# Attention output by full-width streams with ones beside V, and a new order of the first halves' work, in an attention and feed-forward kernel

## The chip, the cores and the metric

The kernel runs on one core of one Trainium2 chip. The metric is the device time of one execution in microseconds; a "fast" run is one that lies within 1.5% of the fastest run of the same kernel. Profiles are of single executions, and their span is some 1.8 us shorter than the time of that execution.

Engines: PE is TensorE, DVE VectorE, ACT ScalarE, POOL GpSimd, SP SyncE (which here only issues transfers). PSUM is the memory into which PE writes its results; a pool's "bufs" are its buffers. A crossbar transpose is a transfer that transposes on its way. PE is called cold where its groups stand about twice as far apart as elsewhere (1.28 us instead of 0.65 for a gate group).

## The reference, cut to what matters

```python
# q, k, v: (4, 8, 768, 64); 8 global keys, 96 local keys
scores = q @ k.T / 8 + bias(head, distance); masked to global | local keys
a = exp(scores - max) / sum(exp(scores - max))
x = (a @ v) regrouped to (3072, 512)
out = (relu(x @ w_gate) * (x @ w_val)) @ w_out      # 512 -> 1536 -> 512
```

The kernel cuts each of the 4 batches into two halves of 384 queries: halves 0 to 7. Chunk c of the feed-forward is half c. While PE works on the feed-forward of chunk c, the attention of half c+1 is woven in between. QK is the product of queries and keys, AV that of the weights and V. A batch's even half is called a first half, its odd half a second half.

## The kernel before

Keys are cut into tiles j of 120 keys of their own and the 8 global ones. For each pair of heads, `piece_qk` makes the unnormalised weights `es`, and `piece_av` runs twice: once with ones as the stationary operand (the sum of the weights), once with V. Each matmul fills 64 of the 128 columns of the array; the two heads of a pair stand in the two halves.

```python
def piece_av(s, p, what):
    av = av_psum.tile([128, 512], FP32, name="av_ps")          # av_psum has 2 buffers
    for i, (j, a, w, m) in enumerate(todo):                    # 4 tiles in a first half, 5 in a second
        for e in range(2):
            nc.tensor.matmul(av3[64 * e : 64 * e + 64, :, a : a + w],
                             lhsT=ones if what == 0 else vbuf[b % 2][:, j, D * h : D * h + D],
                             rhs=es[...], ...)
    if what == 0:
        nc.scalar.activation(ln, av[:, 0:QH], AF.Ln, ...)
        nc.scalar.activation(rc, ln, AF.Exp, bias=0.0, scale=-1.0)
    else:
        nc.vector.tensor_tensor(xT_of[s][:, p, :], av[:, 0:QH], av_of[s, p], op=ALU.mult)
...
# halves 0 and 1: casts, PE transposes (piece_t), copies to qT and kT
# halves 2 to 7 ("early pieces"): casts on GpSimd, crossbar transposes issued by SP, copies to kT on GpSimd
...
weave(f1_0[0:G2], [])
weave(f1_0[G2 : 2 * G2], attention_pieces(1), 0.0, 1.2)
...
weave(f1_1[0 : 2 * G2], [])
weave(f1_0[2 * G2 :] + f1_1[2 * G2 :], early_pieces(2))
weave(f2_0 + f2_1, attention_pieces(2) + early_pieces(3))
```

`weave` emits feed-forward pieces in order and puts the attention pieces between them at even distances. Every engine is given its instructions in the order of the program, so this order decides who waits for whom.

The softmax here doesn't subtract the row's maximum and nothing guards it: scores larger than these inputs give would overflow.

## Time and profile before

The time was 284.66 us in the median of four runs (284.48 to 288.38). The execution that the profile shows took 285.32 us, at a mean granted clock of 0.976.

| engine | busy, us | share of the span of 283.5 us |
|---|---|---|
| PE | 250.5 | 88% |
| PE weight loads | 138.6 | 49% |
| ACT | 147.7 | 52% |
| DVE | 123.0 | 43% |
| POOL | 93.7 | 33% |

PE's 88% is not evenly spread: from 127 us on it has no gap, before that it has holes. Two groups of the page of the kernel before give the price of what follows a pair's AV (line, engine, operation, tiles and shapes, count; then busy us and mean ns of one; then the engine's idle time before them):

```profile
L339 DVE TENSOR_TENSOR xT<-av_ps,rcp 128x384 bf16<-128x384 f32 x32 | 17.8, 555 | 37.2 <-PE av_ps L325 29.9
...
L332 ACT ACTIVATE lnd<-av_ps 128x384 f32<-128x384 f32 x32 | 15.8, 494 | 17.4 <-PE av_ps L325 17.4
```

There is one logarithm of 494 ns and one multiply of 555 ns per pair, each over all 128 partitions.

### The profile page before, as it was taken

Reading aid. Unit: us, or ns where it says so; the run is one execution under the profiler, and the core shown is the slowest. Engines: PE = TensorE matmul, PEld = TensorE weight load, DVE = VectorE, ACT = ScalarE, POOL = GpSimd, SP = SyncE. Lnnn points to the kernel's source line nnn. Section 1 sums busy time; section 2 is a strip of 40 time slices with the busy share of each in tenths; the row PEclk is TensorE's granted clock in tenths of the full one; section 3 lists DMA queues with packets and bytes.
Section 4 is the critical chain, followed back from the end, with each engine's and each line's share of the span. In section 5 each row is a group of like instructions: output and inputs, shape, how many; then the busy total and the mean of one; then the engine's idle time right before and its main releaser. Section 6 shows DMA issues by size and latency. Waiting matters only on the chain.

```text
span 283.5 us, 5047 instructions
## 1 busy us (share of the span) xinstructions
PE 250.5 (88%) x1824; PEld 138.6 (49%) x1824; DVE 123.0 (43%) x328; ACT 147.7 (52%) x301; POOL 93.7 (33%) x231
## 2 busy tenths in 40 slices
PE   1366966799989929999999999999999999999994
PEld 0134534465545415554555455554555465545551
DVE  6555266634344105652355326540664155523320
ACT  8466245833367215664565457554755376543421
POOL 8990129614280019425051631434140300000000
PEclk9997799999999986999999999999999999999999
DMA  7999990998412379747454397348845110011002
GB/s 199 170 204 193 228 237 9 109 287 233 102 39 75 93 190 261 96 109 77 131 172 112 96 148 226 69 100 118 259 58 112 74 39 1 2 62 49 2 22 89
DMA packets 81200, 34.38 MB, mean 121 GB/s; under 512 B 56920, under 2 KB 78104, under 8 KB 81176
## 3 DMA queue, kind: packets, MB, share of 16 engines
q1 hardware_dynamic: 49320, 26.16, 32.9%
q0 software_dynamic: 31856, 7.91, 28.0%
q8 instruction: 14, 0.23, 0.3%
q14 instruction: 10, 0.08, 0.1%
HBM read 28.38 MB, written 6.29 MB: 122 GB/s over the span
## 4 chain that ended last, share of the span: by engine, by line
PE 77%; ACT 7%; DMA 6%; DVE 4%; SPq 3%; issue 1%; POOL 0%; ACTq 0%; DVEq 0%; POOLq 0%
PE ff_ps L375 21%; PE ff_ps L384 21%; PE ff_ps L365 21%; PE av_ps L325 8%; PE qk_ps L298 6%; DMA ks<-in_k_dram 5%; ACT es L301 2%; SPq L271 1%; ACT m_all L208 1%; DVE es L310 1%; SPq L274 1%; DMA kN<-kc 1%; SPq L111 1%; DVE qT L258 1%; ACT lnd L332 1%
## 5 line engine op out<-in xcount | busy, mean ns | idle before, releaser
L375 PE MATMUL ff_ps<-xT,wv 128*128 128x384 bf16 x384 | 80.7, 334 | 0.0
L365 PE MATMUL ff_ps<-xT,wg 128*128 128x384 bf16 x384 | 80.4, 332 | 0.1
L377 DVE TENSOR_TENSOR ht<-ff_ps,grelu 128x384 bf16<-128x384 f32 x96 | 53.3, 555 | 49.2 <-PE ff_ps L375 44.1
L368 ACT ACTIVATE grelu<-ff_ps 128x384 bf16<-128x384 f32 x96 | 47.1, 491 | 48.5 <-PE ff_ps L365 24.6
L384 PE MATMUL ff_ps<-wo_sb,ht 128*128 128x512 bf16 x288 | 67.9, 380 | 0.0
L310 DVE TENSOR_TENSOR es<-es,m_all 128x432 bf16<-128x432 bf16 (+6 forms) x144 | 43.4, 331 | 54.3 <-ACT es L301 52.9
L301 ACT ACTIVATE es<-qk_ps 128x432 bf16<-128x432 f32 (+2 forms) x96 | 49.4, 530 | 23.5 <-PE qk_ps L298 22.0
L298 PE MATMUL qk_ps<-qT,kT 128*128 128x432 bf16 (+6 forms) x144 | 33.9, 304 | 20.7 <-DVE kT L239 8.2
L375 PEld LDWEIGHTS <-wv 128*128 128x128 bf16 x384 | 37.1, 100 | 26.6 <-issue 3.9
L365 PEld LDWEIGHTS <-wg 128*128 128x128 bf16 x384 | 36.3, 99 | 24.6 <-issue 1.8
L384 PEld LDWEIGHTS <-ht 128*128 128x128 bf16 x288 | 26.0, 98 | 28.8
L339 DVE TENSOR_TENSOR xT<-av_ps,rcp 128x384 bf16<-128x384 f32 x32 | 17.8, 555 | 37.2 <-PE av_ps L325 29.9
L389 ACT COPY osb<-ff_ps 128x512 f32<-128x512 f32 x24 | 14.1, 586 | 30.2 <-PE ff_ps L384 30.2
L265 POOL CAST qz<-qs 128x192 bf16<-128x192 f32 x48 | 16.6, 373 | 36.1 <-issue 20.7
L298 PEld LDWEIGHTS <-kT 128*128 128x128 bf16 x144 | 14.0, 101 | 29.5 <-issue 10.0
L332 ACT ACTIVATE lnd<-av_ps 128x384 f32<-128x384 f32 x32 | 15.8, 494 | 17.4 <-PE av_ps L325 17.4
L131 POOL DMA_DIRECT2D vbuf<-in_v_dram x28 | 24.4, 883 | 0.0
L241 POOL COPY kT<-kN 128x240 bf16<-128x240 bf16 x12 | 5.0, 418 | 39.8 <-DMA kN<-kc 39.8
L325 PEld LDWEIGHTS <-ones 128*64 128x64 bf16 x288 | 11.4, 113 | 13.4 <-issue 12.7
L334 ACT ACTIVATE rcp<-lnd 128x384 f32<-128x384 f32 x32 | 16.7, 523 | 1.0
L325 PE MATMUL av_ps<-es,vbuf 128*64 128x216 bf16 (+6 forms) x288 | 15.7, 237 | 1.6 <-ACT lnd L332 1.2
L325 PEld LDWEIGHTS <-vbuf 128*64 128x64 bf16 x288 | 11.6, 114 | 10.1 <-issue 10.1
(60 smaller groups left out, 105.9 us busy)
## 6 DMA issues: line engine op xcount, KB each, us to landing
out_dram<-osb SPq DMA_DIRECT2D x24, 256.0 KB, 2.0
qs<-in_q_dram SPq DMA_DIRECT2D x6, 768.0 KB, 5.9
ks<-in_k_dram SPq DMA_DIRECT2D x6, 768.0 KB, 6.5
vbuf<-in_v_dram POOLq DMA_DIRECT2D x24, 120.0 KB, 4.4
qs<-in_q_dram SPq DMA_DIRECT2D x8, 192.0 KB, 12.8
ks<-in_k_dram SPq DMA_DIRECT2D x8, 192.0 KB, 4.7
wg<-in_moe_w_gate_dram POOLq DMA_DIRECT2D x3, 512.0 KB, 8.2
wv<-in_moe_w_val_dram POOLq DMA_DIRECT2D x3, 512.0 KB, 10.0
```

The source lines that it names most:

```text
L131: nc.gpsimd.dma_start(out=v_dst(b, NG, NG + n, j), in_=v[b, :, KT * j : KT * j + n, :].rearrange("h p d -> p h d"))
L298: nc.tensor.matmul(ps[:, c : c + n_], lhsT=kt[:, j, :], rhs=qd[:, :, :, a : a + w], start=True, stop=True)
L301: nc.scalar.activation(es[:, 0:cols], ps[:, 0:cols], AF.Exp, bias=0.0, scale=scale)
L310: nc.vector.tensor_mul(e4, e4, mk)
L325: nc.tensor.matmul(av3[64 * e : 64 * e + 64, :, a : a + w], lhsT=ones if what == 0 else vbuf[b % 2][:, j, D * h : D * h + D], rhs=es[:, ce ...
L332: nc.scalar.activation(ln, av[:, 0:QH], AF.Ln, bias=0.0, scale=1.0)
L339: nc.vector.tensor_tensor(xT_of[s][:, p, :], av[:, 0:QH], av_of[s, p], op=ALU.mult)
L365: nc.tensor.matmul(psg[:, 0:QH], lhsT=w_of(wg, dc, fc), rhs=xT[:, dc, :], start=(dc == 0), stop=(dc == N_DC - 1))
L368: nc.scalar.activation(gr, psg[:, 0:QH], AF.Relu, bias=0.0, scale=1.0)
L375: nc.tensor.matmul(psv[:, 0:QH], lhsT=w_of(wv, dc, fc), rhs=xT[:, dc, :], start=(dc == 0), stop=(dc == N_DC - 1))
L377: nc.vector.tensor_tensor(ht[:, fc, :], psv[:, 0:QH], st["gr"], op=ALU.mult)
L384: nc.tensor.matmul(ps2, lhsT=ht[:, fc, n * 128 : (n + 1) * 128], rhs=wo_sb[:, fc, :], start=(fc == 0), stop=(fc == N_FC - 1))
```

## The change

Its intent: use the whole width of the array in AV from half 2 on, so that a head needs half as many matmuls; and bring the work of halves 0 to 3 into an order in which engines wait less. The core of the diff:

```diff
-    tp_psum = ... bufs=1;  qk_psum = ... bufs=2
+    qk_psum = ... bufs=3                     # transposes share it
-    vbuf = [const.tile([128, NT, DM], BF16, ...
+    vbuf = [const.tile([128, NT, (2 * H + 1) * D], BF16, ...     # ones | V0 | ones | V1 | ... | ones
...
-            eng = nc.vector if s == 0 and (i == 0 or p == 0) else nc.gpsimd
+            eng = nc.vector if s == 0 else nc.gpsimd
...
-        put_keys(nc.scalar.copy, nc.vector.tensor_copy, kt, tp[:, 1, :], half)
+        put_keys(nc.vector.tensor_copy, nc.vector.tensor_copy, kt, tp[:, 1, :], half)
...
-    def piece_av(s, p, what):
+    def piece_av(s, p, e):                   # one head, 128 columns: V and ones
+        for i, (j, a, w, m) in enumerate(todo):
+            z0 = 2 * D * h + (D if e == 0 else 0)
+            nc.tensor.matmul(av3[:, :, a : a + w], lhsT=vb[:, j, z0 : z0 + 128], rhs=es[...], ...)
+        nc.scalar.activation(ln[o0 : o0 + 64], av[d0 : d0 + 64, 0:QH], AF.Ln, ...)
+        if e == 1:
+            nc.scalar.activation(rc, ln, AF.Exp, bias=0.0, scale=-1.0)
+            for e_ in range(2):
+                nc.vector.tensor_tensor(xT_of[s][r, p, :], av_of[s, p, e_][r, 0:QH], rc[r], op=ALU.mult)
+    def piece_av_wide(s, p): ...             # the old streams, for halves 0 and 1
...
-            return (C(0) + T(0) + C(1) + QK(0) + T(1) + C(2) + QK(1) + T(2) + ...
+            return (C(0) + T(0) + C(1) + T(1) + QK(0) + C(2) + T(2) + QK(1) + C(3) + T(3) + QK(2) + AW(0)
+                    + QK(3) + AW(1) + AW(2) + AW(3))
...
-    weave(f1_0[0:G2], [])
-    weave(f1_0[G2 : 2 * G2], attention_pieces(1), 0.0, 1.2)
+    weave(f1_0[G[0]], spread(attention_pieces(1), 0.1, 1.6),
+          [(0.9, lambda: load_w_group(2)), (0.95, lambda: load_w(wo_sb, moe_w_out, 0, DM))])
...
-    weave(f1_0[2 * G2 :] + f1_1[2 * G2 :], early_pieces(2))
-    weave(f2_0 + f2_1, attention_pieces(2) + early_pieces(3))
+    weave(f1_1[G[0]])
+    weave(f1_0[G[1]] + f1_1[G[1]], spread(early_pieces(2), 0.0, 1.0))
+    weave(f1_0[G[2]] + f1_1[G[2]] + f2_0 + f2_1,
+          spread(attention_pieces(2), 0.3, 0.9), spread(early_pieces(3), 0.4, 0.8))
...
+            placed.append(spread(attention_pieces(c + 1), 0.0, 0.88))
+            placed.append(spread(early_pieces(c + 2), 0.25, 0.75))
```

Cut: fills of the wider V tile with ones, moved loads and memsets.

More of the change, by code (lines that the diff above doesn't have):

```diff
@@ L73 @@
     osb_pool = ctx.enter_context(tc.tile_pool(name="osb", bufs=2))
-    tp_psum = ctx.enter_context(tc.tile_pool(name="tpps", bufs=1, space=bass.MemoryType.PSUM))
-    qk_psum = ctx.enter_context(tc.tile_pool(name="qkps", bufs=2, space=bass.MemoryType.PSUM))
+    qk_psum = ctx.enter_context(tc.tile_pool(name="qkps", bufs=3, space=bass.MemoryType.PSUM))
     av_psum = ctx.enter_context(tc.tile_pool(name="avps", bufs=2, space=bass.MemoryType.PSUM))
@@ L84 @@
     ident = const.tile([128, 128], BF16)
-    vbuf = [const.tile([128, NT, DM], BF16, name=f"vbuf{i}") for i in range(2)]
+    vbuf = [const.tile([128, NT, (2 * H + 1) * D], BF16, name=f"vbuf{i}") for i in range(2)]
     ones = const.tile([128, D], BF16)
@@ L116, in v_dst @@
     def v_dst(b, r0, r1, j):
-        return vbuf[b % 2][r0:r1, j, :].rearrange("p (h d) -> p h d", d=D)
+        t = vbuf[b % 2][r0:r1, j, D:]
+        return t.rearrange("p (h z) -> p h z", z=2 * D)[:, :, 0:D]
     def load_v_globals(b):
@@ L126, in spread_v_globals, with load_v, fill @@
             out=t[0:NG, j0:j1, :],
-            in_=t[0:NG, 0:1, :].to_broadcast([NG, j1 - j0, DM]))
-    def load_v(b, j):
-        n = min(KT, S - KT * j)
+            in_=t[0:NG, 0:1, :].to_broadcast([NG, j1 - j0, (2 * H + 1) * D]))
+    def load_v(b, j, r0=0, r1=KT):
+        n = min(r1, S - KT * j) - r0
         nc.gpsimd.dma_start(
-            out=v_dst(b, NG, NG + n, j),
-            in_=v[b, :, KT * j : KT * j + n, :].rearrange("h p d -> p h d"))
+            out=v_dst(b, NG + r0, NG + r0 + n, j),
+            in_=v[b, :, KT * j + r0 : KT * j + r0 + n, :].rearrange("h p d -> p h d"))
+    def fill(eng, i, j):
+        eng.memset(vbuf[i][:, j, :].bitcast(mybir.dt.uint32), 0x3F803F80)
     def load_v_half(s):
@@ L166 @@
     nc.vector.memset(ones, 1.0)
-    nc.vector.memset(vbuf[0][:, NT - 1, :], 0.0)
+    fill(nc.vector, 0, 0)
     dd = setupp.tile([128, 2, NN, WQ], FP32)
@@ L200 @@
     nc.vector.tensor_scalar(dd[0:NG, 0], gd, BIG, float(NL), op0=ALU.mult, op1=ALU.max)
-    for p in range(HP):
-        nc.vector.memset(kT[0][p][:, 3, 32:128], 0.0)
     for p in range(2):
@@ L248, in piece_t @@
         qk = cast_of[s, p]
-        tp = tp_psum.tile([128, 2, QH], BF16, name="tp")
+        tp = qk_psum.tile([128, 512], FP32, name="qk_ps")
+        tp = tp[:, 0:QH].bitcast(BF16).rearrange("d (i t) -> d i t", i=2)
         for i in range(2):
@@ L312, in piece_qk @@
             c += n_
-    def piece_av(s, p, what):
+    def piece_av(s, p, e):
         b, half = divmod(s, 2)
+        h = 2 * p + e
+        vb = vbuf[b % 2]
         av = av_psum.tile([128, 512], FP32, name="av_ps")
+        av_of[s, p, e] = av
         av3 = av[:, 0:QH].rearrange("d (n p) -> d n p", n=NN)
@@ L321, in piece_av @@
             es, c = es_of[s, p, j]
-            for e in range(2):
-                h = 2 * p + e
-                ce = c + e * NN * w
-                nc.tensor.matmul(av3[64 * e : 64 * e + 64, :, a : a + w],
-                                 lhsT=ones if what == 0 else vbuf[b % 2][:, j, D * h : D * h + D],
-                                 rhs=es[:, ce : ce + NN * w].rearrange("k (n p) -> k n p", n=NN),
-                                 start=(i == 0), stop=(i == len(todo) - 1),
-                                 skip_group_check=True)
@@ L330, in piece_av @@
-        if what == 0:
-            ln = rc_pool.tile([128, QH], FP32, name="lnd")
-            nc.scalar.activation(ln, av[:, 0:QH], AF.Ln, bias=0.0, scale=1.0)
+            c += e * NN * w
+            z0 = 2 * D * h + (D if e == 0 else 0)
+            nc.tensor.matmul(av3[:, :, a : a + w],
+                             lhsT=vb[:, j, z0 : z0 + 128],
+                             rhs=es[:, c : c + NN * w].rearrange("k (n p) -> k n p", n=NN),
+                             start=(i == 0), stop=(i == len(todo) - 1),
+                             skip_group_check=True)
@@ L333, in piece_av @@
+        o0, d0 = (0, 64) if e == 0 else (64, 0)
+        if e == 0:
+            av_of[s, p, "l"] = rc_pool.tile([128, QH], FP32, name="lnd")
+        ln = av_of[s, p, "l"]
+        nc.scalar.activation(ln[o0 : o0 + 64], av[d0 : d0 + 64, 0:QH], AF.Ln, bias=0.0, scale=1.0)
+        if e == 1:
+            if s not in xT_of:
+                xT_of[s] = xt_pool.tile([128, N_DC, QH], BF16, name="xT")
             rc = rc_pool.tile([128, QH], FP32, name="rcp")
             nc.scalar.activation(rc, ln, AF.Exp, bias=0.0, scale=-1.0)
-            av_of[s, p] = rc
-        else:
-            if s not in xT_of:
-                xT_of[s] = xt_pool.tile([128, N_DC, QH], BF16, name="xT")
-            nc.vector.tensor_tensor(xT_of[s][:, p, :], av[:, 0:QH], av_of[s, p], op=ALU.mult)
+            for e_ in range(2):
+                r = slice(64 * e_, 64 * e_ + 64)
+                nc.vector.tensor_tensor(xT_of[s][r, p, :], av_of[s, p, e_][r, 0:QH], rc[r],
+                                        op=ALU.mult)
@@ new lines, in piece_av_wide @@
+    def piece_av_wide(s, p):
+        b, half = divmod(s, 2)
+        todo = [t for bank in banks_of_half[half] for t in bank]
+        av = [av_psum.tile([128, 512], FP32, name="av_ps") for _ in range(2)]
+        for what in range(2):
+            av3 = av[what][:, 0:QH].rearrange("d (n p) -> d n p", n=NN)
+            for i, (j, a, w, m) in enumerate(todo):
+                es, c = es_of[s, p, j]
+                for e in range(2):
+                    z0 = D + 2 * D * (2 * p + e)
+                    ce = c + e * NN * w
+                    nc.tensor.matmul(av3[64 * e : 64 * e + 64, :, a : a + w],
+                                     lhsT=ones if what == 0 else vbuf[b % 2][:, j, z0 : z0 + D],
+                                     rhs=es[:, ce : ce + NN * w].rearrange("k (n p) -> k n p", n=NN),
+                                     start=(i == 0), stop=(i == len(todo) - 1),
+                                     skip_group_check=True)
+        ln = rc_pool.tile([128, QH], FP32, name="lnd")
+        nc.scalar.activation(ln, av[0][:, 0:QH], AF.Ln, bias=0.0, scale=1.0)
+        rc = rc_pool.tile([128, QH], FP32, name="rcp")
+        nc.scalar.activation(rc, ln, AF.Exp, bias=0.0, scale=-1.0)
+        if s not in xT_of:
+            xT_of[s] = xt_pool.tile([128, N_DC, QH], BF16, name="xT")
+        nc.vector.tensor_tensor(xT_of[s][:, p, :], av[1][:, 0:QH], rc, op=ALU.mult)
@@ L343, in attention_pieces @@
         QK = lambda p: [(0.18, lambda g=g: piece_qk(s, p, g)) for g in range(3)]
-        AV = lambda p: [(0.28, lambda e=e: piece_av(s, p, e)) for e in range(2)]
+        AW = lambda p: [(0.58, lambda: piece_av_wide(s, p))]
+        AV = lambda p: [(0.29, lambda e=e: piece_av(s, p, e)) for e in range(2)]
         C = lambda p: [(0.0, lambda: piece_cast(s, p))]
         if s == 0:
-            return (C(0) + T(0) + C(1) + QK(0) + T(1) + C(2) + QK(1) + T(2) + C(3) + QK(2) + AV(0)
-                    + T(3) + AV(1) + QK(3) + AV(2) + AV(3))
-        if s >= 2:
-            return QK(0) + QK(1) + AV(0) + QK(2) + AV(1) + QK(3) + AV(2) + AV(3)
-        return (C(0) + C(1) + T(0) + C(2) + T(1) + C(3) + QK(0) + T(2) + QK(1) + AV(0) + T(3) + QK(2) + AV(1)
-                + QK(3) + AV(2) + AV(3))
+            return (C(0) + T(0) + C(1) + T(1) + QK(0) + C(2) + T(2) + QK(1) + C(3) + T(3) + QK(2) + AW(0)
+                    + QK(3) + AW(1) + AW(2) + AW(3))
+        if s == 1:
+            return (C(0) + T(0) + C(1) + T(1) + QK(0) + C(2) + T(2) + QK(1) + AW(0) + C(3) + T(3) + QK(2) + AW(1)
+                    + QK(3) + AW(2) + AW(3))
+        return QK(0) + QK(1) + AV(0) + QK(2) + AV(1) + QK(3) + AV(2) + AV(3)
     out_v = out.rearrange("(s p n) d -> s n p d", p=128, n=NN)
@@ L400, in ffn_pieces, with spread, weave @@
         return f1, f2
-    def weave(f_items, a_items, first=0.0, last=0.9):
+    def spread(items, first, last):
+        n = len(items)
+        return [(first + (i + 0.5) / n * (last - first), f) for i, (_, f) in enumerate(items)]
+    def weave(f_items, *placed):
         total = sum(t for t, _ in f_items)
+        a_items = sorted((x for p in placed for x in p), key=lambda x: x[0])
         done, ai = 0.0, 0
@@ L408, in weave @@
             done += t
-            while (ai < len(a_items)
-                   and (first + (ai + 0.5) / len(a_items) * (last - first)) * total <= done):
+            while ai < len(a_items) and a_items[ai][0] * total <= done:
                 a_items[ai][1]()
@@ L420 @@
     a0 = attention_pieces(0)
-    pool_work = {
-        0: [lambda: load_v_globals(0), lambda: load_v(0, 0), lambda: load_v(0, 1)],
-        2: [lambda: load_v(0, 2), lambda: spread_v_globals(0, 1, 4)],
-        3: [lambda: load_v(0, 3),
-            lambda: zero_q(0, 2)],
-        7: [lambda: zero_q(0, 3),
-            lambda: load_w_group(0)],
+    aside = {
+        1: [lambda: fill(nc.vector, 0, 1), lambda: fill(nc.vector, 0, 2),
+            lambda: load_v_globals(0), lambda: load_v(0, 0), lambda: load_v(0, 1)],
+        2: [lambda: nc.vector.memset(kT[0][0][:, 3, 32:128], 0.0), lambda: fill(nc.vector, 0, 3),
+            lambda: load_v(0, 2), lambda: spread_v_globals(0, 1, 4)],
+        3: [lambda: load_v(0, 3), lambda: zero_q(0, 2)] +
+           [lambda p=p: nc.vector.memset(kT[0][p][:, 3, 32:128], 0.0) for p in range(1, HP)],
+        7: [lambda: zero_q(0, 3), lambda: load_w_group(0)],
+        13: [lambda: load_qk_after(1, True)],
     }
     for i, (_, f) in enumerate(a0):
-        for g in pool_work.get(i, []):
+        for g in aside.get(i, []):
             g()
         f()
-        if i == len(a0) - 6:
-            load_qk_after(1, True)
-    load_w_group(1)
+    for j in range(4, NT):
+        fill(nc.gpsimd, 0, j)
+    spread_v_globals(0, 4, NT)
     for p in range(HP):
         nc.gpsimd.memset(kT[0][p][:, 6, NG + 48 : 128].bitcast(mybir.dt.uint32), 0)
-    spread_v_globals(0, 4, NT)
     load_v_half(1)
@@ L441 @@
         zero_q(1, p)
-    load_w_group(2)
-    load_w(wo_sb, moe_w_out, 0, DM)
+    load_w_group(1)
     f1_0, f2_0 = ffn_pieces(0)
     f1_1, f2_1 = ffn_pieces(1)
-    G2 = 2 * GW
-    weave(f1_0[0:G2], [])
-    weave(f1_0[G2 : 2 * G2], attention_pieces(1), 0.0, 1.2)
+    G = [slice(2 * GW * i, 2 * GW * (i + 1)) for i in range(N_FC // GW)]
+    weave(f1_0[G[0]], spread(attention_pieces(1), 0.1, 1.6),
+          [(0.9, lambda: load_w_group(2)), (0.95, lambda: load_w(wo_sb, moe_w_out, 0, DM))])
     for p in range(HP):
@@ L452 @@
         nc.gpsimd.memset(kT[1][p][:, 6, NG + 48 : 128].bitcast(mybir.dt.uint32), 0)
-    nc.gpsimd.memset(vbuf[1][:, NT - 1, :].bitcast(mybir.dt.uint32), 0)
+    for j in range(NT):
+        fill(nc.gpsimd, 1, j)
     for i in range(2):
@@ L457 @@
     load_v_half(2)
-    weave(f1_1[0 : 2 * G2], [])
+    weave(f1_1[G[0]])
+    weave(f1_0[G[1]] + f1_1[G[1]], spread(early_pieces(2), 0.0, 1.0))
     load_qk(3, 0, H)
     load_v_half(3)
-    weave(f1_0[2 * G2 :] + f1_1[2 * G2 :], early_pieces(2))
-    weave(f2_0 + f2_1, attention_pieces(2) + early_pieces(3))
+    weave(f1_0[G[2]] + f1_1[G[2]] + f2_0 + f2_1,
+          spread(attention_pieces(2), 0.3, 0.9), spread(early_pieces(3), 0.4, 0.8))
     for c in range(2, NHALF):
-        early = []
+        placed = []
+        if c + 1 < NHALF:
+            placed.append(spread(attention_pieces(c + 1), 0.0, 0.88))
         if c + 2 < NHALF:
@@ L468 @@
             load_v_half(c + 2)
-            early = early_pieces(c + 2)
+            placed.append(spread(early_pieces(c + 2), 0.25, 0.75))
         f1, f2 = ffn_pieces(c)
-        a_ = attention_pieces(c + 1) if c + 1 < NHALF else []
-        items = []
-        for i in range(max(len(a_), len(early))):
-            items += a_[i : i + 1]
-            if i >= 8:
-                items += early[i - 8 : i - 7]
-        items += early[max(0, len(a_) - 8):] if len(early) > len(a_) - 8 else []
-        weave(f1 + f2, items)
+        weave(f1 + f2, *placed)
 _INS = ['q', 'k', 'v', 'n_global', 'n_local', 'moe_w_gate', 'moe_w_val', 'moe_w_out']
```

## The prediction

> **What bounds the kernel now.** I read the busy time by stretch first, cutting the span where the tensor engine (PE) changes its work: attention of half 0, its first feed-forward groups with attention of half 1, feed-forward alone, attention of half 2, then one stretch per half (columns: stretch, length, busy us of each engine with its instruction count, granted clock, DMA share, GB/s).
>
> ```profile
> 4.30:27.50 23.20, 11.83 (x105) 7.65 (x105) 12.25 (x41) 14.52 (x32) 16.40 (x33) 0.95 1.45 200
> 27.50:56.40 28.90, 22.16 (x196) 12.74 (x193) 16.40 (x51) 14.54 (x32) 14.15 (x27) 0.92 1.02 149
> 56.40:76.60 20.20, 20.20 (x126) 12.18 (x125) 8.37 (x15) 7.86 (x16) 4.92 (x15) 1.00 0.81 219
> 76.60:99.30 22.70, 21.08 (x153) 10.52 (x152) 7.76 (x21) 11.92 (x25) 7.49 (x23) 1.00 0.21 65
> 99.30:127.50 28.20, 22.98 (x157) 12.84 (x156) 12.36 (x32) 14.01 (x28) 13.65 (x36) 0.88 0.85 165
> 127.50:157.20 29.70, 29.70 (x223) 16.23 (x221) 13.11 (x32) 17.07 (x35) 8.65 (x21) 1.00 0.57 126
> ...
> 187.10:216.70 29.60, 29.60 (x222) 16.21 (x221) 13.13 (x31) 17.06 (x35) 10.20 (x27) 1.00 0.63 129
> ```
>
> From 127.5 us on PE has no gap; VectorE (DVE) and ScalarE (ACT) are near half busy. There only less PE work saves time. Before that PE has holes, and waits and order count. The timeline of PE in a full stretch prices the work:
>
> ```profile
> 201.90 0.81 PE L365 MATMUL ff_ps<-xT,wg 128*128 128x384 bf16 x4
> 202.64 0.45 PE L325 MATMUL av_ps<-es,ones 128*64 128x216 bf16 x8
> 203.03 0.82 PE L375 MATMUL ff_ps<-xT,wv 128*128 128x384 bf16 x4
> 203.78 0.45 PE L325 MATMUL av_ps<-es,vbuf 128*64 128x216 bf16 x8
> 204.16 0.82 PE L365 MATMUL ff_ps<-xT,wg 128*128 128x384 bf16 x4
> 204.82 0.35 PE L298 MATMUL qk_ps<-qT,kT 128*128 128x432 bf16 x1
> 205.00 0.81 PE L375 MATMUL ff_ps<-xT,wv 128*128 128x384 bf16 x4
> ```
>
> Starts tell the cost: a gate or value group to its equal neighbour takes 0.65 us; with one AV piece of 8 matmuls between, 203.03 - 201.90 = 1.13 and 204.16 - 203.03 = 1.13, so the piece costs 0.48. In a second half (10 matmuls) the output groups of 1.29 us stand 1.82 apart (187.05, 188.87, 190.71), so 0.53. A QK matmul of 432 columns costs 0.18, exactly its columns.
>
> The other large loss is at 99 us. Lines of the timelines of SyncE (SP), GpSimd (POOL) and PE:
>
> ```profile
> 81.06 14.22 SPq L390 DMA_DIRECT2D out_dram<-osb  x4
> 95.39 1.29 SPq L271 DMA_TRANSPOSE qT<-qz  x1
> ```
> ```profile
> 83.58 0.50 POOL L266 CAST kc<-ks 128x384 bf16<-128x384 f32 x1
> 105.16 0.42 POOL L241 COPY kT<-kN 128x240 bf16<-128x240 bf16 x1 [21.07 <-DMA kN<-kc]
> ```
> ```profile
> 104.22 0.28 PE L298 MATMUL qk_ps<-qT,kT 128*128 128x144 bf16 x1 [4.09 <-DMA qT<-qz]
> 105.63 0.46 PE L298 MATMUL qk_ps<-qT,kT 128*128 128x336 bf16 x1 [1.13 <-POOL kT L241]
> 105.88 1.49 PE L375 MATMUL ff_ps<-xT,wv 128*128 128x384 bf16 x4
> ```
>
> The casts of half 3 are done at 84, but its crossbar transposes queue on SP behind output writes that wait for their results, and start at 95.4. PE stands still, then runs cold.
>
> **What the Trainium skill says.** "TensorEngine Tiling (Array Packing)", Key Properties, says a change of tiling mode drains the engine, and its Restrictions say column tiling turns off the fast weight load. The trace fits: an AV piece starts 0.74 us after a group of 0.65, and its 8 half-wide matmuls, in pairs covering 600 columns, cost 0.48 where 600 columns at the QK rate (0.18/432) are 0.25. "TensorE: Matmul & The Clock Gate", Part 1, says an idle window of about 3.4 us halves the clock and about as much activity restores it: after the 4.09 us wait groups start 1.28 us apart (plus QK) instead of 0.65 until 110. "DMA: Bandwidth & Descriptors", Queues, rings and completion order, says the engines alternate between queue rows they have work for; the q and k loads of half 1, issued at 25.1 to 32.2 with weights in flight, feed casts one per 2.05 us, 192 KB each, some 96 GB/s, about half of the 200 shown.
>
> **The change part by part.**
>
> *AV, halves 2 to 7.* Removed: per pair of heads, two column-halved streams. Added: two full-wide streams, with ones beside V. Columns per head are the same, 600 (first half) or 3 x (24+64+72+56+16) = 696 (second), but there are 4 or 5 matmuls per piece instead of 8 or 10. At the QK rate a piece is 0.27 or 0.30 us (with a few ns per matmul). Saved per pair 2 x (0.48 - 0.27) = 0.42, or 2 x (0.53 - 0.30) = 0.46; per half 1.7 or 1.8; three of each, 10.5 us of PE where PE is the bound. Off PE: one more Ln (0.49 us) and one more normalising multiply (0.555) per pair, assuming duration follows columns and not partitions; 4 x 0.5 on each engine in a half of 28 us, so ACT about 68% and DVE about 54% busy.
>
> *The new wait.* The AV tile of the even head is now free only after the odd head's Ln, Exp and the multiply. In the gate region the next pair is over 5 us away. In the output region the order of instructions puts pair 2's two heads together, one output group (1.29), then pair 3. Chain from the end of pair 2: output copy 0.59 (may stand before), Ln 0.49, Ln 0.49 (the first partly overlapped), Exp 0.52, multiply 0.555, handovers 0.2: 2.1 to 2.3 us. Against 1.29: 0.7 to 1.0 us of PE waiting once per half. Halves 3 to 7: 5 x 0.85 = 4.3; in half 2 pair 3's heads stand together and wait for both multiplies, about 1.3.
>
> *Half 0.* Before, PE's first feed-forward matmul is at 27.5. Key copies move to DVE, so the first no longer waits for the eight mask exponentials on ACT (kT copied at 7.64; free at about 6). But DVE now carries 8 casts (3.0 us), fills (2.1), query copies (8 x 0.35), key copies (4 x (0.43+0.18+0.19), the first an estimate from ACT's time), masks (5.6), normalising (2.2): 18.9 us from 4.0 on. Casts of pair p+1 precede its transpose, for whose 0.8 us cold PE time DVE waits, three times; the last three AV pieces then chain through Ln, Exp and multiply. By hand along the DVE queue I get the last multiply at about 27 and the first gate matmul at about 26: 1.5 us gained.
>
> *Half 1.* Its loads are now issued at about 17.6 (after the last casts of half 0, by the DVE order) instead of 25.1, and the last weight group and output weights only after its casts. Its data land by about 29 instead of 42. Then DVE is the bound: 4 ht products 2.2, query copies 2.8, key copies 3.2, masks 6.3, normalising 2.2 = 16.7, plus about 4 of waits like those of half 0: 26 + 20.7, say 46.7. Only 8 feed-forward groups (5.2 us) lie beside it; before, 16 did, to 56.4. On equal work the before would stand there at 46.7 + 5.2 = 51.9: gain 4.5, including the 1.5.
>
> *Half 2 and the stall.* Then PE alone: chunk 1's first groups 5.2, second groups 10.4, third groups 10.4, outputs 15.6, QK 2.0, AV 4 x 0.545 = 2.2, wait 1.3: 46.7 + 47.1 = 93.8, against 99.3 before. Half 2's loads go out at about 47; before, the way from issue (56.2) to the first key copy (76.8) took 20.6, so its keys are there at 68, and its QK starts 30% into the last stage at 62.3 + 7.8 = 70: just in time. Half 3's transposes now sit behind two output writes only, about 80; 8 us of crossbar and 4 of ordering give its keys at 90 to 93. So the stretch 99.3 to 127.5 loses its hole: 4.09 + 1.13 + about 3 x 0.63 cold + 0.8 in slower QK = 8 us.
>
> *Sum.* 284.7 - 5.5 (to the start of chunk 2) - 8 (stall) - (3 x 1.8 + 2 x 1.7 = 8.8) + 4.3 = 265.7, say 266.
>
> **The rivals.** (1) *The gain of AV is eaten by the longer chain.* For: DVE sits in order, and its two multiplies now wait for Exp of the odd head, about 1.2 us with ht products behind them; ff has 3 buffers. Against: walking the slots, each is free just before PE wants it. If each of four pairs cost 0.5 us, 5 halves x 2 = 10 us back: 275. (2) *DVE becomes the bound in the first halves beyond my sum*, the dense stage after it unchanged: for, 18.9 of 23 us there; against, POOL loses its casts. A further 2 us per half: 270. (3) *The stall only moves*: half 2 or 3 is short of keys by a few us, since my margins are 0 to 3 us; 269, or 272 with cold PE. (4) *The AV wait is hidden* because Ln of the even head overlaps more and copies stand elsewhere: 262.
>
> **Range and chances.** The AV saving and the stall are each read from a row and worth over 15 us together; rivals 1 to 3 would have to come all together to leave under 2% (5.7 us). Misses on both sides of 2 to 5 us are likely: 261 to 271. Faster 0.97, same 0.02, slower 0.01.
>
> **What would show it.** Right: AV pieces cost 0.27 to 0.30 between groups, a full stretch is about 28.8 instead of 29.6, one PE wait of 0.7 to 1.0 us named for the normalising multiply per stretch; no wait for the crossbar near 94; PE clock 1.00 from 50 on; first gate matmul near 26, attention of half 1 done near 47 with DVE over 75% busy from 26 to 47. Wrong: AV pieces near 0.4 (the drain was not the cost), PE waits on ff tiles after each odd head, Ln or multiplies on 64 partitions much cheaper or dearer than on 128, or first key waits in halves 2 and 3.

## The result, and the profile after

The changed kernel takes 268.55 us in the median of four runs (267.58 to 270.11), the kernel before 284.66 us. Ratios are the mean time of one kernel's fast runs over that of the other's of the same rounds, so not quite the ratio of these medians: here 0.941 (95% interval 0.932 to 0.950). The outcome is faster by 5.9%; 268.55 lies inside the predicted range and 2.5 us above the predicted 266.0.

The stretches of the changed kernel that answer to those of before (same columns: stretch, length, busy us of PE, PE weight load, DVE, ACT and POOL with their counts, granted clock, DMA share, GB/s):

```profile
4.30:26.00 21.70, 12.14 (x105) 7.74 (x105) 17.11 (x55) 12.78 (x28) 16.08 (x34) 1.00 1.40 207
26.00:42.30 16.30, 14.29 (x161) 8.93 (x158) 14.21 (x48) 11.38 (x25) 11.96 (x26) 1.00 0.93 168
42.30:66.90 24.60, 24.20 (x150) 14.37 (x148) 10.43 (x21) 9.24 (x19) 8.12 (x17) 1.00 1.08 171
66.90:69.70 2.80, 0.16 (x2) 0.00 (x0) 0.18 (x1) 0.49 (x1) 0.90 (x4) 1.00 0.55 96
69.70:92.40 22.70, 22.11 (x133) 11.74 (x134) 9.76 (x25) 14.73 (x30) 13.12 (x37) 1.00 0.80 191
92.40:122.30 29.90, 28.55 (x194) 16.93 (x193) 16.88 (x42) 19.55 (x39) 13.88 (x32) 1.00 0.77 140
122.30:151.20 28.90, 27.91 (x181) 16.31 (x180) 15.20 (x37) 18.91 (x39) 10.36 (x29) 1.00 0.68 134
151.20:180.60 29.40, 28.47 (x194) 17.00 (x193) 15.75 (x41) 19.55 (x39) 8.08 (x23) 1.00 0.71 141
```

The column of the granted clock does not show the cold start: in the first row it is 1.00, and yet six transposes take 0.61 us from start to start (7.92 to 8.53), and 0.34 later (27.71 to 28.05).

The reader is to see four things. The first gate matmul now comes at 26.0 instead of 27.5, and attention of half 1 ends at 42.3. There is a new hole of 2.8 us at 66.9. Chunk 2 starts at 92.4 instead of 99.3, and its stretch has shrunk from 38.1 (99.3 to the start of chunk 3 at 137.5) to 29.9. A full stretch takes 28.9 or 29.4; before, chunks 3 to 6 took 29.3, 30.2, 29.4 and 29.8 (starts at 137.46, 166.78, 196.97, 226.37 and 256.19).

So the 17.3 us between the two spans (283.5 and 266.2) came thus: at the start of chunk 2 the changed kernel is 7.0 ahead, at that of chunk 3 137.46 - 122.29 = 15.2, and the four stretches after it add 2.2. Most of the gain is in the first third. The spans lie further apart than the medians (16.1), as the execution shown of the kernel before ran at a clock of 0.976 and that of the changed one (267.93 us) at 1.00. Some 2.3 us of the 7.0 are a cold start that is gone: before, the first four feed-forward groups stand 1.26, 1.27, 1.28 and 1.11 apart (27.49 to 32.41), and in the changed kernel they are at 0.65 from 27.06 on. The prediction's parts do not name this.

PE in a full stretch, from its timeline:

```profile
130.47 0.42 PE L327 MATMUL av_ps<-es,vbuf 128*128 128x216 bf16 x4
130.74 0.81 PE L407 MATMUL ff_ps<-xT,wv 128*128 128x384 bf16 x4
131.39 0.42 PE L327 MATMUL av_ps<-es,vbuf 128*128 128x216 bf16 x4
131.67 0.81 PE L397 MATMUL ff_ps<-xT,wg 128*128 128x384 bf16 x4
```

From start to start an AV piece costs 0.27 us (130.47 to 130.74), as predicted, and the value group its plain 0.65: the late start of 0.09 is gone too. In a second half a piece costs 0.30 (101.27 to 101.57).

Now the output region of the same stretch, lines of the timeline of all engines, the busy ones of the AV chain:

```profile
143.78 0.70 PE L327 MATMUL av_ps<-es,vbuf 128*128 128x216 bf16 x8
143.98 0.59 ACT L421 COPY osb<-ff_ps 128x512 f32<-128x512 f32 x1 [0.85 <-PE ff_ps L416]
...
144.33 1.46 PE L416 MATMUL ff_ps<-wo_sb,ht 128*128 128x512 bf16 x6
144.59 1.00 ACT L336 ACTIVATE lnd<-av_ps 64x384 f32<-64x384 f32 x2
...
145.62 0.52 ACT L341 ACTIVATE rcp<-lnd 128x384 f32<-128x384 f32 x1
146.17 1.14 DVE L344 TENSOR_TENSOR xT<-av_ps,rcp 64x384 bf16<-64x384 f32 x2 [2.61 <-ACT rcp L341]
146.78 0.42 PE L327 MATMUL av_ps<-es,vbuf 128*128 128x216 bf16 x4 [0.99 <-DVE xT L344]
```

The output copy goes first on ACT, then two logarithms, the exponential, the first multiply; PE's next AV piece starts when that multiply has freed its tile. An output group lasts 1.29 us from start to start, so PE could have gone on at 144.33 + 1.29 = 145.62 and went on at 146.78: 1.16 us lost. In the stretches with a second half it is 1.09 (117.80 instead of 116.71).

The hole at 66.9, lines of the timeline:

```profile
66.25 0.81 PE L397 MATMUL ff_ps<-xT,wg 128*128 128x384 bf16 x4
...
68.80 0.54 POOL L237 COPY kT<-kN 128x360 bf16<-128x360 bf16 x1 [8.77 <-DMA kN<-kc]
...
69.43 0.23 POOL L239 COPY kT<-kT 128x56 bf16<-128x56 bf16 x1
...
69.71 0.36 PE L299 MATMUL qk_ps<-qT,kT 128*128 128x432 bf16 x1 [2.65 <-POOL kT L239]
```

The first QK of half 2 stands in PE's stream at 66.9, but its keys are copied only at 69.65, at the end of a chain: q and k loads issued at 43.3, k landed at 56.3, casts to 60.0, six crossbar transposes to 68.7, copies.

The groups of the page that answer to those shown of before:

```profile
L344 DVE TENSOR_TENSOR xT<-av_ps,rcp 64x384 bf16<-64x384 f32 x48 | 26.7, 555 | 43.7 <-ACT rcp L341 43.0
...
L336 ACT ACTIVATE lnd<-av_ps 64x384 f32<-64x384 f32 x48 | 23.3, 486 | 9.7 <-PE av_ps L327 8.9
```

Over 64 partitions one multiply still takes 555 ns and one logarithm 486 instead of 494: here the duration follows the 384 columns. DVE, which formerly waited for PE before the multiply, now waits for the exponential.

### The profile page after: what moved, and what is told of

Read it like the earlier page. It is cut to its first block, busy times and chain, and to the rows that moved or that the text cites. A ratio compares the mean times of both kernels' runs of the same rounds, so it can differ in the third digit from the quotient of the medians.

```text
span 266.2 us, 4655 instructions
## 1 busy us (share of the span) xinstructions
PE 237.6 (89%) x1608; PEld 139.1 (52%) x1608; DVE 140.8 (53%) x366; ACT 156.8 (59%) x317; POOL 97.2 (37%) x237
## 4 chain that ended last, share of the span: by engine, by line
PE 71%; DVE 9%; DMA 6%; ACT 6%; SPq 2%; POOL 2%; issue 2%; DVEq 0%; ACTq 0%; POOLq 0%
PE ff_ps L416 20%; PE ff_ps L407 19%; PE ff_ps L397 19%; PE qk_ps L299 6%; PE av_ps L327 5%; DMA ks<-in_k_dram 5%; ACT lnd L336 2%; DVE xT L344 1%; DVE es L311 1%; DVE kT L239 1%; PE av_ps L359 1%; PE qk_ps L253 1%; SPq L272 1%; ACT rcp L341 1%; SPq L275 1%
## 5 line engine op out<-in xcount | busy, mean ns | idle before, releaser
L397 PE MATMUL ff_ps<-xT,wg 128*128 128x384 bf16 x384 | 78.5, 326 | 1.1 <-DVE xT L344 0.4
L407 PE MATMUL ff_ps<-xT,wv 128*128 128x384 bf16 x384 | 78.0, 326 | 0.0
L302 ACT ACTIVATE es<-qk_ps 128x432 bf16<-128x432 f32 (+2 forms) x96 | 49.4, 529 | 28.3 <-PE qk_ps L299 25.9
L311 DVE TENSOR_TENSOR es<-es,m_all 128x432 bf16<-128x432 bf16 (+6 forms) x144 | 43.3, 392 | 29.5 <-ACT es L302 28.7
L344 DVE TENSOR_TENSOR xT<-av_ps,rcp 64x384 bf16<-64x384 f32 x48 | 26.7, 555 | 43.7 <-ACT rcp L341 43.0
L416 PEld LDWEIGHTS <-ht 128*128 128x128 bf16 x288 | 26.9, 97 | 27.7
L336 ACT ACTIVATE lnd<-av_ps 64x384 f32<-64x384 f32 x48 | 23.3, 486 | 9.7 <-PE av_ps L327 8.9
L421 ACT COPY osb<-ff_ps 128x512 f32<-128x512 f32 x24 | 14.1, 586 | 25.1 <-PE ff_ps L416 23.3
L327 PE MATMUL av_ps<-es,vbuf 128*128 128x216 bf16 (+4 forms) x216 | 20.6, 225 | 5.4 <-DVE xT L344 5.4
L327 PEld LDWEIGHTS <-vbuf 128*128 128x128 bf16 x216 | 17.6, 97 | 13.6 <-issue 6.9
L299 PEld LDWEIGHTS <-kT 128*128 128x128 bf16 x144 | 14.3, 102 | 16.1 <-issue 3.8
L267 POOL CAST kc<-ks 128x384 bf16<-128x384 f32 x24 | 12.7, 531 | 13.3 <-DMA ks<-in_k_dram 13.3
L253 PE MATMUL qk_ps<-ident,qk 128*128 128x128 bf16 x48 | 5.5, 264 | 12.0 <-DVE qk L222 12.0
L237 POOL COPY kT<-kN 128x360 bf16<-128x360 bf16 x12 | 6.4, 537 | 26.1 <-DMA kN<-kc 26.1
```

What stands on the lines that cost most here:

```text
L299: nc.tensor.matmul(ps[:, c : c + n_], lhsT=kt[:, j, :], rhs=qd[:, :, :, a : a + w], start=True, stop=True)
L302: nc.scalar.activation(es[:, 0:cols], ps[:, 0:cols], AF.Exp, bias=0.0, scale=scale)
L311: nc.vector.tensor_mul(e4, e4, mk)
L327: nc.tensor.matmul(av3[:, :, a : a + w], lhsT=vb[:, j, z0 : z0 + 128], rhs=es[:, c : c + NN * w].rearrange("k (n p) -> k n p", n=NN), star ...
L336: nc.scalar.activation(ln[o0 : o0 + 64], av[d0 : d0 + 64, 0:QH], AF.Ln, bias=0.0, scale=1.0)
L344: nc.vector.tensor_tensor(xT_of[s][r, p, :], av_of[s, p, e_][r, 0:QH], rc[r], op=ALU.mult)
```

## The experiments

Eleven kernels were run in three groups, each on one chip, beside the kernel before. Across groups, compare ratios to the kernel before; its medians were 286.09, 285.25 and 285.60 us. Every kernel gave correct results.

### The baseline, and its clock

> The changed kernel once more, on the chip of the next three runs, as their baseline. Both theories: 267.5 to 270 us, because its four runs on record spread from 267.58 to 270.11.

It took 269.27 us (ratio 0.9406). Its runs, 269.2 to 269.9, had a mean granted clock of 0.987 or 0.994; in the first four runs of the same kernel, those at clock 1.00 took 267.6 and 267.9, those at 0.99 took 269.2 and 270.1. The profile of this run shows the same hole (2.76 us) and then, in the PE timeline, cold groups:

```profile
71.68 1.45 PE L407 MATMUL ff_ps<-xT,wv 128*128 128x384 bf16 x4
72.93 0.63 PE L416 MATMUL ff_ps<-wo_sb,ht 128*128 128x512 bf16 x1
```

The value group takes 1.25 us from start to start instead of 0.65. In the profile above, after a hole of 2.65 us, it took 0.65. From the first QK to the start of chunk 2 it took 24.3 us here and 22.6 there. So the hole sometimes costs its 2.8 us and sometimes some 1.7 more.

### The AV change alone, taken back

```diff
-        AV = lambda p: [(0.29, lambda e=e: piece_av(s, p, e)) for e in range(2)]
+        AV = lambda p: [(0.29, lambda e=e: piece_av_narrow(s, p, e)) for e in range(2)]   # old streams, V at its new place
```

> The changed kernel with the old AV in halves 2 to 7 (ones and V by column halves, same places in the stream, one Ln and one multiply less per pair); all of the new order kept. Theory (the wide stream saves 10.5 us of PE time, the longer chain gives back about 7): AV pieces cost 0.48 and 0.53 us again, the 1.1 us waits for the multiply vanish, 2.5 to 4.5 us slower than the changed kernel, 271.5 to 274. Rival (the wide stream brings nothing beside the order): within 1 us of 269. Rival (the chain's waits are not on the path): 8 us or more slower.

Measured: 270.79 us, ratio 0.9473, against 0.9406: 0.7% or nearly 2 us slower, below the expected 2.5 to 4.5. The intervals of the two ratios overlap, so the stretches have to decide. They took 29.1 and 29.8 (starts 122.66, 151.77, 181.59), against 28.9 and 29.4: as it stands, the wide stream nets some 0.2 to 0.5 us per stretch, 1.3 over the four from chunk 3 on. Of the 16 us of the whole change some 2 are its own, by this run; the rest goes with the new order. The waits for the multiply are gone here, as the theory has it. What the expectation missed: in the order of the new kernel pair 2's two narrow streams stand next to each other, and such a double piece costs 0.84 us (output groups start at 173.19 and 175.32, less 1.29), not 2 x 0.53. That is some 0.24 more than two wide pieces (2 x 0.30), about the 0.23 that a single narrow piece costs more than a wide one. So what the narrow streams cost beside their columns goes with each change to column halves and back, not with each matmul.

### Pair 2's AV sooner

```diff
+        out = spread(attention_pieces(s), first, last)
+        for i in (16, 17):                    # the two heads of pair 2
+            out[i] = (at + 0.0001 * i, out[i][1])
...
-            placed.append(spread(attention_pieces(c + 1), 0.0, 0.88))
+            placed.append(attention_placed(c + 1, 0.0, 0.88, 0.714))
```

Half 2's stage likewise, at 0.79.

> Only the AV of pair 2 stands one output group earlier (right behind the last QK piece), so that two output groups, 2.6 us, lie between it and pair 3; unlike the earlier trial no QK piece is moved behind the key copies of the next half. Theory (the chain of 2.3 to 2.5 us from pair 2's AV to the freed tile is what PE waits for): no wait for the multiply of 0.9 us is left in halves 3 to 7, 5 to 6 us less than the changed kernel, 263.5 to 264.5. Rival (PE waits as long for another step): under 2 us gained.

Measured: 263.75 us, ratio 0.923: some 1.9% or 5 us better than the changed kernel. Not one wait for the multiply is left in halves 3 to 7, and the stretches take 27.8 and 28.3 (starts 120.81, 148.56, 176.82). The PE timeline has two output groups from 141.54 on, and then, with no wait named and 2 x 1.29 us later, pair 3:

```profile
144.13 0.42 PE L327 MATMUL av_ps<-es,vbuf 128*128 128x216 bf16 x4
```

The theory holds. Against the narrow streams' 29.1 and 29.8 the wide stream is worth 1.4 and 1.6 us per stretch when nothing waits for its longer chain.

### A buffer more for AV

```diff
-    qk_psum = ... name="qkps", bufs=3      av_psum = ... name="avps", bufs=2
+    qk_psum = ... name="qkps", bufs=2      av_psum = ... name="avps", bufs=3
```

> The changed kernel with three PSUM buffers for AV and two for QK and transposes (three and two before, the other way round). Theory (the AV wait is a wait for a buffer): the 0.9 us waits for the multiply go in halves 3 to 7, worth 5 us, but the first halves, whose transposes and QK pieces share the two buffers, lose 1 to 4 us; 265 to 268. Rival (buffers do not matter for AV): 269 or more with the same AV waits.

Measured: 264.87 us, ratio 0.928, just under the expected 265 to 268. The stretches are 27.8 and 28.3 as in the run before, with no AV wait: the wait is one for a buffer. The first halves pay: PE waits for the exponentials with the two QK buffers (five waits of 0.66 to 0.77 us between 31 and 42), and half 1's last AV piece starts at 43.53 instead of 41.84.

### Pair 3's QK behind pair 2's AV: an order that ran into a dependency

```diff
-        return QK(0) + QK(1) + AV(0) + QK(2) + AV(1) + QK(3) + AV(2) + AV(3)
+        return QK(0) + QK(1) + AV(0) + QK(2) + AV(1) + QK(3)[:1] + AV(2) + QK(3)[1:] + AV(3)
```

> Same instructions, but two of pair 3's three QK pieces stand between the AV of pair 2 and that of pair 3. Theory (the wait of pair 3's AV for the normalising multiply of pair 2, 1.1 us per half, is fully on the path): the waits in halves 3 to 7 go (5 x 1.13 = 5.6 us) and most of half 2's 1.5, so 5 to 7 us less than the changed kernel. Rival (the AV of the next pair or the gate groups wait for the same chain elsewhere, now between pair 1 and pair 2): less than 2 us gained, and the trace shows new waits for the multiply in the gate region.

Measured: 280.23 us, ratio 0.977: 11 us slower. Neither theory said this. The AV waits did go in the stretches in which a second half's attention runs. In the others PE waits for something new (one line of three of the kind, PE timeline):

```profile
153.96 0.20 PE L299 MATMUL qk_ps<-qT,kT 128*128 128x48 bf16 x1 [3.37 <-POOL kT L242]
```

Key tile 3 is shared by a batch's two halves. With its last QK piece moved behind the key copies of the next half in program order, the QK of the first half reads what those copies write, and waits for the whole crossbar chain: 4.17, 3.37 and 3.94 us at 93.7, 154.0 and 215.9, with a cold clock after. The result stays right, since the mask removes those keys. The experiment says nothing against the AV theory; the two runs above, which leave the QK pieces in place, tested it cleanly.

### Half 3's key work late again

```diff
-          spread(attention_pieces(2), 0.3, 0.9), spread(early_pieces(3), 0.4, 0.8))
+          spread(attention_pieces(2), 0.3, 0.9), spread(early_pieces(3), 0.93, 0.99))
```

> Only the casts, crossbar transposes and ordering of half 3 are moved in program order to the end of the output stage, behind five output writes. Theory (the old stall at 99 us came from the crossbar issue standing behind output writes on SyncE): the stall returns, PE waits 5 to 7 us for the crossbar or the key copies near 94 us and then runs some 2 us cold, 276 to 279 us. Rival (the stall was the late load of half 3 or slow casts): under 2 us slower.

Measured: 280.84 us, ratio 0.983: 11.6 us slower than 269.27, more than expected. The timelines of SP and PE:

```profile
77.51 17.54 SPq L422 DMA_DIRECT2D out_dram<-osb  x6
95.15 1.30 SPq L272 DMA_TRANSPOSE qT<-qz  x1
```
```profile
103.39 0.28 PE L299 MATMUL qk_ps<-qT,kT 128*128 128x144 bf16 x1 [8.68 <-DMA qT<-qz]
```

The casts of half 3 are done at 79.5, and the crossbar starts at 95.15 behind six output writes: the stall of the kernel before, from this one placement. It is deeper (8.68 and 1.06 us instead of 4.09 and 1.13) because PE now arrives at 93.9 instead of 99.3, while the crossbar is as late as it was.

### The output weights later

```diff
-          [(0.9, lambda: load_w_group(2)), (0.95, lambda: load_w(wo_sb, moe_w_out, 0, DM))])
+          [(0.9, lambda: load_w_group(2))])
...
-    weave(f1_0[G[1]] + f1_1[G[1]], spread(early_pieces(2), 0.0, 1.0))
+    weave(f1_0[G[1]] + f1_1[G[1]], spread(early_pieces(2), 0.0, 1.0), [(0.4, lambda: load_w(wo_sb, moe_w_out, 0, DM))])
```

> The load of the output weights is issued after the casts of half 2 instead of before its q and k loads. Theory (the 2.8 us wait of half 2's first QK at 66.9 comes from q and k loads that share the DMA engines with the output weights: k took 12.5 us to land): k lands in 6 to 9 us, the keys are ready some 3 to 5 us earlier, the wait goes, 2.5 to 3 us less. Rival (casts, crossbar and ordering alone are too long for the place of this attention in the stage): the wait stays over 1.5 us and the time within 1 us.

Measured: 276.39 us, ratio 0.9645, 7 us slower; the hole grew to 8.92 us. The first casts of k could start at 54.0 instead of 56.4, so the loads did come sooner; but the weights, issued at 57.5, then ran beside the transposes (SP timeline):

```profile
59.98 4.30 SPq L272 DMA_TRANSPOSE qT<-qz  x1
...
67.22 4.88 SPq L272 DMA_TRANSPOSE qT<-qz  x1
```

Where a transpose holds SP for 1.3 us in the changed kernel, it held it for 2.9 to 4.9 here, and the key copies began at 74.7 instead of 68.8. The theory named one contention and the edit put a worse one in its place; by how much the output weights delay the loads of half 2 stays open beyond the 2.4 us seen.

### Attention of half 2 later

```diff
-          spread(attention_pieces(2), 0.3, 0.9), spread(early_pieces(3), 0.4, 0.8))
+          spread(attention_pieces(2), 0.4, 0.9), spread(early_pieces(3), 0.4, 0.85))
```

> Attention of half 2 starts at 0.4 of its stage instead of 0.3 (and the key work of half 3 ends at 0.85 instead of 0.8). Theory (the 2.8 us wait for half 2's keys at 66.9 is a matter of its place, nothing later needs it so early): the wait goes, 1 to 2.8 us less, part of it lost because ScalarE has to do the same work in less time. Rival (attention of half 2 is then the bound of its stage): the same time within 1 us or slower, with new waits on the exponentials.

Measured: 264.95 us, ratio 0.927: 1.4% or about 4 us better than the changed kernel. The hole is gone, and all six runs have a clock of 0.997 to 1.00. So the gain is more than the 2.8 us of the hole because the cold clock after it goes too: between two executions at clock 1.00, this one of 265.03 us and the changed kernel's of 267.93 from the first four runs, it is 2.9 us. ScalarE kept up.

### Half 1's key copies back on ScalarE

```diff
-        put_keys(nc.vector.tensor_copy, nc.vector.tensor_copy, kt, tp[:, 1, :], half)
+        put_keys(nc.vector.tensor_copy if s == 0 else nc.scalar.copy, nc.vector.tensor_copy, kt, tp[:, 1, :], half)
```

> Only the large key copies of half 1 go back from VectorE to ScalarE. Theory (VectorE, 99% busy from 30 to 40 us, is the bound of half 1's attention): 4 x 0.41 us leave it, the first gate matmul after that attention (42.3) comes 1 to 1.6 us earlier, and so do half 2's loads and keys; 1 to 1.5 us less in all. Rival (the chain of transpose, copy, QK, exponential is the bound, and the copy behind other ScalarE work only lengthens it): within 0.5 us or slower.

Measured: 269.29 us, ratio 0.941: the same. The rival was right about the stage: DVE's share from 30 to 40 us fell from 99% to 76%, PE waited 2.1 us twice for exponentials, and half 1's last AV piece started at 45.16 instead of 41.84, 3.3 us later. But the total did not move, and the 2.65 us hole for half 2's keys vanished. The end of half 1's attention has about 3 us of slack against the arrival of half 2's keys: in the changed kernel, finishing it early only lengthens the hole. The load of k was issued 3.0 us later here (46.84 instead of 43.80), and yet its first cast began at 56.63 instead of 56.41: its issue does not set when k lands; probably the transfers in front of it do.

### V's fills on ScalarE

```diff
-    for j in range(4, NT):
-        fill(nc.gpsimd, 0, j)
+        # after half 0's first QK pieces, for j in 4, 5, 6:
+        nc.scalar.copy(vbuf[0][:, j, :]..., ones.unsqueeze(1).to_broadcast([128, 2 * H + 1, D]))
```

> The three fills of V tiles 4 to 6 are done by ScalarE, idle then, instead of GpSimd. Theory (the VectorE cast of half 0's pair 2, 2.5 us instead of 0.35 at 11.07 to 13.6, was held by GpSimd's three 128x544 memsets at 11.5 to 13.1): the cast takes under 1 us, the transpose of pair 2 starts at 11.5 to 12.5 instead of 13.63, the first gate matmul comes 1 to 2 us earlier, and the end 1 to 2 us earlier if the loads of half 1 and 2 follow. Rival (the cast waits for its DMA or the stretch is an artefact of the record): transpose of pair 2 still at 13.3 to 13.9, time the same.

Measured: 267.36 us, ratio 0.9337 against 0.9406: 0.7% or 1.9 us better. The cast of pair 2 in the changed kernel and here (DVE and POOL timelines of the changed kernel, then DVE of this one):

```profile
11.07 2.51 DVE L222 CAST qk<-qs 128x384 bf16<-128x384 f32 x1
```
```profile
11.52 1.56 POOL L136 MEMSET vbuf<- 128x544 uint32 x3
```
```profile
11.08 0.64 DVE L222 CAST qk<-qs 128x384 bf16<-128x384 f32 x1
```

With the three memsets gone the cast takes 0.64 instead of 2.51 us, though POOL still issues transfers at that time, and PE's transpose of pair 2 starts at 11.78 instead of 13.63, the first gate matmul at 24.33 instead of 26.00. The total follows here, unlike in the run before this one, as the later loads come sooner too: that of the output weights is issued at 32.42 instead of 34.27, that of k at 41.40 instead of 43.80, and the first cast of k begins at 54.10. In the changed kernel a copy and the mask products just before the cast are drawn to 13.4 too, so the record does not tell which of them was held first. "SBUF — State Buffer", Terms, of the Trainium skill says VectorE and GpSimd share a port pair by an exclusive lock and the loser "fully blocks"; the run agrees.

### Three edits together

> Three edits together: fills on ScalarE, AV of pair 2 one output group earlier, attention of half 2 from 0.4 of its stage. Theory (they act on three different waits): 1.9 + 5.5 + about 3.5 less than the changed kernel's 269.3, so 257.5 to 260. Rival (they overlap, or one uncovers the next wait): 261 or more.

Measured: 256.98 us (256.44 to 258.03), ratio 0.899 (0.895 to 0.903). This beats both kernels: 10.1% faster than before and some 12 us faster than the changed one. It is a shade better than the sum of the three gains. The starts of its last chunks lie 27.8 and 28.3 us apart (115.98, 143.73, 172.00), and between 42 and 228 us the profile names one wait of PE, 0.18 us.

## Why the prediction was right or wrong

**AV.** Right in mechanism and piece cost: 0.27 and 0.30 us measured against 0.27 and 0.30 predicted; the narrow streams still cost what the prediction read. The assumption that duration follows columns, not partitions, was right. The gain by half without waits was put at 1.7 or 1.8; 1.4 and 1.6 was measured against the narrow streams in the same order, in which pair 2's streams stand side by side and cost 0.2 less.

**The new wait.** Right in cause, place and count. Its size was set too low: "0.7 to 1.0 us of PE waiting once per half" measured 1.09 to 1.16 from start to start (0.93 to 0.99 as the trace states it), because the output copy stands first on ACT every time and PE resumes a little after the release. In half 2 the waits, with the one of the next gate group, came to about 1.5 instead of 1.3. That is the first mis-sized term: 5 x 0.28 = 1.4 us. So a half nets 0.2 to 0.5 us of the wide stream and not the 0.9 that the prediction's 1.7 or 1.8 less 0.85 leaves.

**Half 0.** Right: first gate matmul at 26.0, and DVE was indeed busy 17.1 of 21.7 us. But part of DVE's time there was not work: the port lock held one cast for over 2 us, which nothing in the prediction's sum shows. Without it the first gate matmul came at 24.33. The predicted and the measured time agree by errors that cancel, and that is luck.

**Half 1.** The predicted 46.7 was 43.3 for the last multiply, with the next gate matmul at 42.3. "Then DVE is the bound" was right, 9.9 of 10 us busy from 30 to 40. Two terms failed. From 26.0 to 43.3 DVE was busy for 14.8 us where the sum has 16.7, and idle for 2.5 where it has "plus about 4 of waits like those of half 0". That feed-forward groups and casts on POOL fill the waits is likely, but no run tested it. The error did not show in the result, since the stretch behind it has slack of that size: the run with key copies on ScalarE lost 3.3 us there and nothing in all. A reading was wrong too: the q and k loads' 96 GB/s are not half of the 200 shown, which belong to the stretch before; from 28 to 42 us, when the loads ran, 238 GB/s were moved. And by 56.4 the kernel before had done 17 groups, not 16; neither figure enters the sum.

**Half 2's keys.** The step that failed is "its keys are there at 68, and its QK starts ... at 70: just in time". The way from issue to keys was taken over from the kernel before, 20.6 us, and took 26.3 (43.3 to 69.65); k alone took 12.5 us to land among other loads, where it had taken 6.7 before. By the earlier end of half 1 PE came at 66.9: 2.8 us of hole, with 1.7 more in the run whose clock dropped. Rival 3 had named this ("half 2 or 3 is short of keys by a few us"), and a first key wait in half 2 stands in the prediction's own list of signs of being wrong; the sum did not carry it.

**The stall at 99.** Right: its stretch lost 8.2 us (38.1 to 29.9) against a predicted 8, and putting one placement back brought the stall back.

**What stays argued.** No run takes back the new order of halves 0 and 1. That the earlier loads of half 1 (issued at 17.7 instead of 25.1) and its shorter attention bring the 7.0 us up to chunk 2 is read from the traces alone; the run with key copies on ScalarE shows only that those copies do not.

**The sum.** The numbers in the prediction's "Sum" add up to 266.7, not 265.7. Against it, chunk 2 starts 1.4 us before the predicted 93.8, the five stretches take 146.5 (92.35 to 238.81) instead of 156.9 - 8 - 8.8 + 4.3 = 144.4, and tail and launch, 29.1, stand 0.6 above the 28.5 of before: 1.2 together, hence 267.9, the time of the execution shown. The remaining 0.6 us to the median are the runs with a lower clock. That chunk 2 came so near to its predicted start is luck as well: half 1 ended 4.4 us early, and the hole and a wait of 0.4 us took back 3.0. Rival 1 failed in the gate region, where no PE wait for the chain appears in a full stretch; its mechanism took hold only in the output region. Rival 2 failed: DVE was the bound of half 1, but for less time than the sum had. Rival 4 failed.

## What to carry to other kernels

When two streams become one with a longer chain behind it, count the buffers by the time from the last matmul to the release, and put that much other work between, above all where pieces stand close together; here moving two pieces by one group brought back more than the change had gained in those stretches. A queue that issues transfers in order is a resource like an engine: a transfer that waits for a result must not stand ahead of one that others need soon. An order change has to be checked for reads that it moves behind writes of shared tiles.

## What the Trainium skill lacked or had wrong

- "TensorEngine Tiling (Array Packing)", Key Properties, gives no size for the drain at a change of mode. Here a first half's piece (600 columns) costs 0.48 us by column halves and 0.27 at full width, a second half's (696) 0.53 and 0.30, and two column-half pieces of a second half side by side cost 0.84. So a change to column halves and back costs some 0.21 to 0.24 us, whether 8, 10 or 20 matmuls stand in between. That this is the drain is inferred.
- "TensorE: Matmul & The Clock Gate", Part 1, speaks of an idle window of about 3.4 us, and Why this matters for your kernels says "No PE-idle gaps >~3µs between matmul bursts". Here shorter holes were enough: those of 2.72 us (the run with fills on ScalarE) and 2.76 us (the baseline) were followed within 1.5 us by some 3 us of cold groups, those of 2.65 us (the changed kernel) and 2.69 us (the AV change taken back) by none. What decides between them stays open.
- "DMA: Bandwidth & Descriptors", DMA Transpose (X-bar), gives no time for transposes beside other traffic. With a weight load in flight one held its queue 2.9 to 4.9 us instead of 1.3.
- "SBUF — State Buffer", SBUF: two separate sides, says the lock is held for one instruction. A VectorE cast was held through GpSimd's three memsets in a row, over 2 us, so it seems that a train of instructions can keep the other engine out.
